# A two-stage kernel (a gated recurrence, then a multiplicative feed-forward): state tiles without zero halves, the diagonal term on TensorE, transposes by DMA, another planner table

## The chip, the cores and the metric

The kernel runs on one core of a Trainium2 chip. The time is the device time of one execution in microseconds; the median of three runs of the kernel before is 220.44 us (220.21 to 220.77). Five engines run side by side, each with its own instruction queue in program order: TensorE (PE), VectorE (DVE), ScalarE (ACT), GpSimd (POOL) and SyncE (SP). POOL and SP also issue the DMA transfers: POOL those that convert f32 to bf16 on the way, SP the others.

## The reference

```python
B, H, S, D = (4, 8, 768, 48)
state = zeros((B, H, D, D))
for t in range(S):
    cur = einsum('bhd,bhe->bhde', u[None] * k[t], v[t])
    y[t] = einsum('bhd,bhde->bhe', r[t], state + cur)
    state = w[t][..., None] * state + einsum('bhd,bhe->bhde', k[t], v[t])
x = y.transpose(0, 2, 1, 3).reshape(B * S, H * D)        # 3072 x 384
out = ((x @ w1) * (x @ w2)) @ w3 @ w_out                 # w1, w2: 384 x 1024, w3: 1024 x 1024, w_out: 1024 x 384
```

## The kernel before

The recurrence is computed in chunks of 128 time steps. Within a chunk the decay is a running sum of logarithms, so that the chunk becomes matrix products: scaled keys times scaled queries (128 x 128 for each batch row and head, strictly causal by a mask), that times v, plus the queries times the state that entered the chunk, plus the diagonal term dv = v * sum(r * u * k).

The work is cut into 12 units (`unit(t)`): 6 chunks of time by 2 pairs of batch rows. A unit holds 2 batch rows x 8 heads x 48 = 768 columns on 128 partitions (time steps). Its steps, by the tile that they write:

- four loads: win (f32, issued by SP), kin, rin and vin (converted to bf16, issued by POOL);
- lw = log w (ACT); cs, the running sum (PE); iw, NEt and Et, three exponentials (ACT); rw, KR's k half and KR's r half, three bf16 products (DVE);
- rk = r*k (DVE, f32), ruk = rk*u (POOL), dg, its sum over 48 (DVE), dv = v*dg (POOL);
- 16 PE transposes of KR into PSUM (L443), one ACT copy of them to KRT (L448);
- per batch row, 8 matmuls of 128 x 128 (L460) and one DVE product with the mask (Mbf, L466); then the matmuls of y (L480 state part, L484 rest), the sum with dv (yb, L491), and PE transposes (L502) and an ACT copy to xT;
- the state: matmuls L519 for two heads at a time, which give a 96 x 96 square of which only the two diagonal 48 x 48 squares are wanted; Tst = that + Sst (DVE, 768 columns); Sbd, the two diagonal squares decayed (POOL, two instructions of 48 partitions); Sst, the whole decayed (POOL, 768 columns).

Two units make a block (`block(n)`, 512 tokens): 8 groups of 3 + 3 matmuls of 512 columns (a, L555, with w1; b, L560, with w2), an ACT copy of a (a_sb, L568), a DVE product (abT, L572); then 4 tiles of 8 matmuls with w34 (L579), an ACT or DVE copy (osb, L586) and a store by SP. The product w34 = w3 @ w_out is made once (`w34_block`): PE transposes of w3 (L354), copies, matmuls with w_out (L366).

Nothing is issued in the order of this text. Each step is declared with an engine, a guessed duration, what it reads and writes, and a priority; `schedule` simulates the engines and always starts the ready step of lowest priority number; the instructions are then issued to the queues in that order. `RANK` shifts the priority of a kind of step, `WEIGHTS_AT` says when each weight is loaded. The planner's numbers set the order alone, never a time on the chip. Between the engines the tile framework puts semaphore waits where data or a buffer needs them. All PSUM is one tile of eight banks (`banks`).

Of the kernel before, what the change touches and what calls it, by code (L numbers as in the profile page):

```python
# [19 lines left out]
    "ne": 35.0, "o": 585.9, "ones": 266.0, "osb": 287.5, "pads": 788.5, "pc": -715.7, "rin": 68.6,  # L20
    "rk": 96.2, "ruk": -33.8, "rw": 700.7, "state": 148.5, "store": -729.5, "table": -999.7, "tr": -53.7,
    "u": 929.4, "vin": 136.2, "w": 156.1, "w3T": 873.0, "win": -499.7, "wm": 844.5, "wt": 733.0, "xT": 70.4,
    "y": 82.9, "yb": -619.8, "yt": -970.4,
}

WEIGHTS_AT = {
    "w1": 9.47, "w2": 28.57, "w3a": 0.47, "w3b": 1.91, "wo": 1.05,
}


class Op:
    __slots__ = ("eng", "dur", "fn", "reads", "writes", "prio", "deps", "tiles", "seq",
                 "start", "end", "lat", "dma", "name", "nleft", "users")

    def __init__(self, eng, dur, fn, reads, writes, prio, lat, dma, name, seq):
        self.eng, self.dur, self.fn = eng, dur, fn
        self.reads, self.writes, self.prio = reads, writes, prio
        self.lat, self.dma, self.name, self.seq = lat, dma, name, seq
        self.deps, self.tiles, self.users = set(), [], []
        self.start = self.end = None  # L40


class Program:
# [39 lines left out]
    def schedule(self, caps):  # L83
# [12 lines left out]
        dma_at = 1500.0  # L96
# [16 lines left out]
        while len(order) < n:  # L113
# [5 lines left out]
            for e, pool in pools.items():  # L119
# [3 lines left out]
                for o in pool:  # L123
                    if ready_at[o] > t or (best is not None and (o.prio, o.seq) >= (best.prio, best.seq)):
                        continue
# [13 lines left out]
                o.start, clock[e] = t, t + o.dur  # L139
                if o.dma:  # L140
                    dma_at = max(dma_at, t + o.dur + 1000.0) + o.dma
                    o.end = dma_at + 1200.0
                else:
                    o.end = t + o.dur
# [6 lines left out]
                for u in o.users:  # L151
                    waiting[u] -= 1
                    lat = 0.0 if (u.eng == e and not o.dma) else o.lat
# [8 lines left out]
            nxt += [f[0] for f in frees if f[0] > t]  # L162
            assert nxt, "the schedule cannot go on"
# [9 lines left out]
def kernel(  # L173
# [27 lines left out]
    NU = NC * NP  # L201
    TB = NP * NB * C
# [18 lines left out]
    KR = many(NS, [C, 2, BH, PAD], BF, "KR")  # L221
    KRT = many(NS, [P, 2, NB, HP, C], BF, "KRT")
    Mbf = many(2 * NS, [C, 2, HP, C], BF, "Mbf")
    rk = many(NS, [C, BH, D], F32, "rk")
    ruk = many(NS, [C, BH, D], F32, "ruk")
    dg = many(NS, [C, BH], F32, "dg")
    dv = many(NS, [C, BH, D], BF, "dv")
    yb = many(2 * NS, [C, DM], BF, "yb")
    pc = many(2 * NP, [P, NB, HP], F32, "pc")
    Tst = many(NP, [P, NB, HP, 2 * D], F32, "Tst")  # L230
    Sst = many(NP, [P, NB, HP, 2 * D], F32, "Sst")
    Sbd = many(NP, [P, NB, HP, 2 * D], BF, "Sbd")
# [16 lines left out]
    u_bc = sb.tile([C, H, D], F32, name="u_bc")  # L249
# [5 lines left out]
    def mm(*cols):  # L255
        return sum(max(n / 2.4 + 2.5, 42.0) for n in cols)

    def act(n):
        return 175 + 0.835 * n

    def dve(n, x=1):
        return 90 + 1.05 * n / x

    def pool(n):
        return 200 + 2.1 * n
# [29 lines left out]
    def c_state():  # L295
        for x in Sbd + Sst:
            nc.vector.memset(x, 0.0)
    op("DVE", 400, c_ones, w=["ones", "LT", "I128"], prio=-10, name="ones")
    op("POOL", 300, c_lt, w=["LT"], prio=-42, name="LT")
    op("POOL", 300, c_id, w=["I128"], prio=-41, name="I128")  # L300
# [3 lines left out]
    op("DVE", 2500, c_state, w=[f"S{i}" for i in range(NP)] + [f"Sbd{i}" for i in range(NP)], prio=-7, name="state0")  # L304
    op("POOL", 1100, c_mask, w=["mask"], prio=-40, name="mask")
    op("SP", 60, lambda: nc.sync.dma_start(u_bc, u.partition_broadcast(C)), w=["u"], prio=-5.0, dma=600.0, name="u")
# [4 lines left out]
    def load(eng, dst, key, src, t, prio, dur):  # L311
        c, p = divmod(t, NP)
        ap = ROW[src][p * NB:(p + 1) * NB, :, c * C:(c + 1) * C, :].rearrange("b h t d -> t (b h) d")
        e = nc.gpsimd if eng == "POOL" else nc.sync
        op(eng, dur, lambda: e.dma_start(dst, ap), w=[key], prio=prio, dma=BH * C * (0.8 if eng == "POOL" else 0.85))  # L315

    def wload(dst, src, key, prio, nbytes):
        op("POOL", 950, lambda: nc.gpsimd.dma_start(dst, src), w=[key], prio=prio, dma=nbytes / 381.0)
# [4 lines left out]
    wor = moe_w_out.rearrange("(gi gp) o -> gp gi o", gp=P)  # L323

# [311 lines left out]
```

## Time and profile before

| | |
|---|---|
| median of the runs | 220.44 us |
| the profiled execution | 221.23 us, of which 219.5 us are the span from first to last instruction |
| PE busy | 165.2 us, 1536 matmuls |
| DVE busy | 147.6 us, 198 instructions |
| POOL busy | 118.5 us, 100 instructions (its DMA issues counted) |
| ACT busy | 108.5 us, 151 instructions |
| DMA | 21.41 MB moved, 27.98 MB read from HBM |

The busy times overlap. An engine's share is a mean over stages: the stretch until the first matmul of a block, and what comes after, have different limits, so the profile is best read stretch by stretch. A POOL row with DMA_DIRECT2D is the time that POOL takes to issue a transfer, not the transfer. The pace of PE is best read from the chain of work, where "x3" rows give three matmuls back to back; the duration of a single matmul includes its latency, of which the next one hides most.

### The profile page before, as it was taken

What the parts mean: (1) busy time and instruction counts of PE and PEld (TensorE: products, weight loads), DVE (VectorE), ACT (ScalarE), POOL (GpSimd) and SP (SyncE); (2) the same over time, 40 slices, a digit from 0 to 9 for tenths busy, and PEclk for the clock granted to TensorE, in tenths of its full rate; (3) what the DMA queues carried; (4) which work ended last, traced back from release to release, by engine and by line L of the source; (5) the groups of instructions that cost most, each with busy time, mean ns of one, the idle gap of its engine ahead of it and who ended that gap; (6) DMA issues with size and microseconds to landing.
All of it is one profiled execution on the core that took longest, in us unless ns stands there. A gap on an engine that the chain in (4) does not pass through costs nothing.

```text
span 219.5 us, 3845 instructions
## 1 busy us (share of the span) xinstructions
PE 165.2 (75%) x1536; PEld 99.9 (46%) x1536; DVE 147.6 (67%) x198; ACT 108.5 (49%) x151; POOL 118.5 (54%) x100
## 2 busy tenths in 40 slices
PE   0060092999457998948899579988879999999993
PEld 0060042676244345535347444476434865464451
DVE  7021014689378299999999999689985698543521
ACT  2061083648570646877458515496534745435410
POOL 7933226189999176976869859766920531000000
PEclk9996557699975599999999999999999999999999
DMA  7999999999999909294669274996280021001033
GB/s 113 181 135 186 153 140 202 138 163 194 160 135 144 139 6 140 75 175 115 36 36 110 73 71 54 105 60 96 21 101 3 0 75 37 3 36 72 0 109 109
DMA packets 105585, 21.41 MB, mean 98 GB/s; under 512 B 99552, under 2 KB 103776, under 8 KB 105568
## 3 DMA queue, kind: packets, MB, share of 16 engines
q0 software_dynamic: 77200, 11.54, 72.7%
q1 hardware_dynamic: 28368, 9.64, 22.1%
q8 instruction: 12, 0.20, 0.4%
q14 instruction: 5, 0.04, 0.1%
HBM read 27.98 MB, written 4.72 MB: 149 GB/s over the span
## 4 chain that ended last, share of the span: by engine, by line
PE 38%; DVE 33%; DMA 10%; issue 9%; POOL 6%; ACT 2%; DVEq 0%; POOLq 0%; ACTq 0%
PE banks L560 11%; DMA vin<-in_v_dram 10%; PE banks L555 10%; DVE Mbf L466 7%; PE banks L579 7%; DVE KR L419 5%; PE banks L443 4%; DVE abT L572 3%; DVE yb L491 3%; DVE rk L425 3%; DVE dg L432 3%; DVE rw L400 3%; PE banks L366 2%; DVE Tst L527 2%; DVE osb L586 1%
## 5 line engine op out<-in xcount | busy, mean ns | idle before, releaser
L572 DVE TENSOR_TENSOR abT<-a_sb,banks 128x512 bf16<-128x512 f32 x48 | 32.5, 682 | 20.1 <-PE banks L560 12.4
L568 ACT COPY a_sb<-banks 128x512 f32<-128x512 f32 x48 | 28.1, 586 | 32.3 <-PE banks L555 32.1
L560 PE MATMUL banks<-xT,w_bf 128*128 128x512 bf16 x144 | 40.3, 389 | 2.2 <-DVE abT L572 2.2
L555 PE MATMUL banks<-xT,w_bf 128*128 128x512 bf16 x144 | 40.4, 390 | 1.0 <-DVE abT L572 0.9
L579 PE MATMUL banks<-w,abT 128*128 128x384 bf16 x192 | 34.0, 326 | 2.2 <-DVE osb L586 2.1
L466 DVE TENSOR_TENSOR Mbf<-banks,mask 128x1024 bf16<-128x1024 f32 x24 | 28.5, 1214 | 4.8 <-PE banks L460 4.8
L428 POOL TENSOR_TENSOR ruk<-rk,u_bc 128x768 f32<-128x768 f32 x12 | 22.5, 1872 | 15.7 <-DVE rk L425 15.6
L534 POOL TENSOR_TENSOR Sbd<-Tst,pc 48x384 bf16<-48x384 f32 x20 | 18.1, 906 | 18.5 <-PE banks L480 17.7
L448 ACT COPY KRT<-banks 128x2048 bf16<-128x2048 bf16 x12 | 22.3, 1867 | 8.9 <-PE banks L443 8.1
L579 PEld LDWEIGHTS <-abT 128*128 128x128 bf16 x192 | 17.9, 98 | 13.3 <-issue 2.3
L560 PEld LDWEIGHTS <-w_bf 128*128 128x128 bf16 x144 | 14.3, 100 | 20.9 <-issue 5.5
L555 PEld LDWEIGHTS <-w_bf 128*128 128x128 bf16 x144 | 14.4, 101 | 18.4 <-issue 3.3
L433 POOL TENSOR_TENSOR dv<-vin,dg 128x768 bf16<-128x768 bf16 x12 | 19.1, 1590 | 4.9 <-issue 2.1
L315 POOL DMA_DIRECT2D vin<-in_v_dram x12 | 14.2, 1185 | 7.6 <-DMA wo_bf<-in_moe_w_out_dram 4.3
L315 POOL DMA_DIRECT2D kin<-in_k_dram x12 | 14.0, 1168 | 7.9 <-DMA vin<-in_v_dram 4.6
L390 PE MATMUL banks<-lw,LT 128*128 128x384 bf16 x24 | 6.5, 356 | 14.0 <-POOL LT L273 12.6
L409 ACT ACTIVATE Et<-banks 128x768 bf16<-128x768 f32 x12 | 9.7, 812 | 14.6 <-PE banks L393 14.6
L508 ACT COPY xT<-banks 128x768 bf16<-128x768 bf16 x12 | 9.6, 802 | 14.0 <-PE banks L502 14.0
L315 POOL DMA_DIRECT2D rin<-in_r_dram x12 | 14.2, 1185 | 3.3 <-DMA rin<-in_r_dram 3.3
L425 DVE TENSOR_TENSOR rk<-rin,kin 128x768 f32<-128x768 bf16 x12 | 13.2, 1102 | 3.7 <-DMA kin<-in_k_dram 3.7
L586 ACT COPY osb<-banks 128x384 f32<-128x384 f32 x12 | 5.8, 481 | 19.4 <-PE banks L579 19.4
L491 DVE TENSOR_TENSOR yb<-banks,dv 128x384 bf16<-128x384 f32 x24 | 12.6, 548 | 4.1 <-POOL dv L433 3.8
(52 smaller groups left out, 260.0 us busy)
## 6 DMA issues: line engine op xcount, KB each, us to landing
win<-in_w_dram SPq DMA_DIRECT2D x12, 384.0 KB, 10.4
out_dram<-osb SPq DMA_DIRECT2D x24, 192.0 KB, 1.9
rin<-in_r_dram POOLq DMA_DIRECT2D x12, 192.0 KB, 7.6
kin<-in_k_dram POOLq DMA_DIRECT2D x12, 192.0 KB, 6.6
vin<-in_v_dram POOLq DMA_DIRECT2D x12, 192.0 KB, 7.8
w_bf<-in_moe_w_dram POOLq DMA_DIRECT2D x2, 1024.0 KB, 19.3
w_bf<-in_moe_w_dram POOLq DMA_DIRECT2D x2, 768.0 KB, 19.4
wo_bf<-in_moe_w_out_dram POOLq DMA_DIRECT2D x1, 768.0 KB, 19.4
```

What stands on the lines that cost most here:

```text
L315: op(eng, dur, lambda: e.dma_start(dst, ap), w=[key], prio=prio, dma=BH * C * (0.8 if eng == "POOL" else 0.85))
L425: op("DVE", dve(BH * D, 2), lambda: nc.vector.tensor_mul(rk[s], rr, kk), r=[kr, kk_], w=[f"rk{s}"], prio=pr + 8)
L428: nc.gpsimd.tensor_mul(ruk[s].rearrange("t (b h) d -> t b h d", b=NB), rk[s].rearrange("t (b h) d -> t b h d", b=NB), u_bc[:, None, :, :]. ...
L433: op("POOL", pool(BH * D), lambda: nc.gpsimd.tensor_mul(dv[s], vv, dg[s][:, :, None].to_broadcast([C, BH, D])), r=[f"dg{s}", kv], w=[f"dv{ ...
L448: nc.scalar.copy(KRTs.rearrange("p x b q t -> p (x b q t)"), o)
L466: nc.vector.tensor_mul(Mbf[m].rearrange("s j q t -> s (j q t)"), o.rearrange("s j f -> s (j f)"), mask.rearrange("s q t -> s (q t)"))
L491: nc.vector.tensor_add(yb[n], banks[:, g.at(Y), :][:, :DM], dv[s][:, b * H:(b + 1) * H, :].rearrange("t h d -> t (h d)"))
L555: nc.tensor.matmul(banks[:, g.at(A), :], lhsT=wt[:, di, fi * P:(fi + 1) * P], rhs=xT[x][:, di, :], start=(di == 0), stop=(di == DI - 1))
L560: nc.tensor.matmul(banks[:, g.at(Bk), :], lhsT=wt[:, di, fi * P:(fi + 1) * P], rhs=xT[x][:, di, :], start=(di == 0), stop=(di == DI - 1))
L568: nc.scalar.copy(a_sb[sa], banks[:, g.at(A), :])
L572: nc.vector.tensor_mul(abT[x][:, fi, :], a_sb[sa], banks[:, g.at(Bk), :])
L579: nc.tensor.matmul(banks[:, g.at(O), :][:, :DM], lhsT=abT[x][:, fi, tt * P:(tt + 1) * P], rhs=w34[:, fi, :], start=(fi == 0), stop=(fi == ...
```

## The change

- **State.** The state keeps two heads one above the other (partitions 0 to 63 and 64 to 127) with 48 columns each, instead of a 96 x 96 square: Tst, Sst and Sbf (formerly Sbd) have 384 columns for a full unit instead of 768. The state matmuls (L758) and the state part of y (L716) are one per head, on halves of the array, 48 columns each: 160 and 160 where there were 80 and 80.
- **Diagonal term.** rk becomes bf16. In units 3 to 12 a DMA transpose issued by SP (L626) turns rk into rkT, six small matmuls with u in block form (u_blk, L633, 8 columns each) give the sums, and a copy of 16 columns (L638) brings them to dg. In units 0 to 2 ruk = rk*u is on DVE in bf16 and the sum stays on DVE. u itself comes through POOL in bf16.
- **Transposes of KR.** In units 6 to 12 two DMA transposes issued by SP (L653) write KRT; the PE transposes and the ACT copy go. Units 0 to 5 keep them.
- **Masks.** For the second batch row of units 5 to 12 ACT copies the product to Mbf (L692) and POOL zeroes it where the mask is zero (affine_select, L695); the other 16 keep the DVE product.
- **Loads.** All loads but the first win go through POOL, in an order that `LOADS` and `STEP` give; w1, w2 are loaded in two halves each, w3 in four quarters.
- **Units and blocks.** The first pair of rows at the first chunk becomes two units of one row (384 columns): 13 units, 8 blocks of 128, 128, 256 and five times 512 tokens. yb, y and its sum are one instruction for both rows. osb copies can go to either engine by a table (`ENGINE`): DVE 5, ACT 19, where there were 12 and 12.
- **Planner.** Other guessed durations, a number for every single step (`STEP`), a model of the port that DVE and POOL share, and two DMA queues in it.

```diff
+STEP = {
+    "table": 6260, "ones": -2200, "LT": -1.5, "pads": -1144, "mask1": 677, "state0": 1306, "mask": 7.5, "u": -10,
...
+LOADS = """win_0 kin_0 rin_0 vin_0 w1_0 w2_0 win_1 kin_1 rin_1 vin_1 u w1_1 w2_1 win_2 kin_2 rin_2 vin_2 wo w3_0 w3_1
+win_3 kin_3 rin_3 vin_3 w3_2 w3_3""".split()
+UNITS = [(0, 0, 1), (0, 1, 1), (0, 2, 2)] + [(c, b, 2) for c in range(1, 6) for b in (0, 2)]
+DMA_KR = set(range(6, 13))
+PE_DIAG = set(range(3, 13))
+POOL_MASK = {(t, 1) for t in range(5, 13)}
+BLOCKS = [[0], [1], [2], [3, 4], [5, 6], [7, 8], [9, 10], [11, 12]]
+SP_LOADS = {("w", 0)}
...
-    rk = many(NS, [C, BH, D], F32, "rk")
+    rk = many(NS, [C, BH, D], BF, "rk")
-    Tst = many(NP, [P, NB, HP, 2 * D], F32, "Tst")
+    Tst = many(NP, [P, NB * HP, D], F32, "Tst")
...
-        op("POOL", pool(BH * D), ruk_, r=[f"rk{s}", "u"], w=[f"ruk{s}"], prio=pr + 8)
+        if t in PE_DIAG:
+            op("SP", 400, lambda: nc.sync.dma_start_transpose(rkTs, rks.rearrange("t h d -> t (h d)")),
...
+                        nc.tensor.matmul(banks[:, g.at(DG), b * H:(b + 1) * H], lhsT=rkTs[:, b * DI + di, :],
+                                         rhs=u_blk[:, di, :], start=(di == 0), stop=(di == DI - 1))
...
+                (nc.scalar.copy if eng == "ACT" else nc.vector.tensor_copy)(dgs, banks[:, g.at(DG), :bh])
...
+        if t in DMA_KR:
+            for x in range(2):
+                def trd(x=x):
+                    nc.sync.dma_start_transpose(KRTs[:, x].rearrange("p b q t -> p (b q) t"),
+                                                KRs[:, x].rearrange("t h d -> t (h d)"))
...
+            if (t, b) in POOL_MASK:
+                op("ACT", act(1024), mcp, r=[MM], w=[f"M{m}"], prio=pr + 7 + b, name=f"mcp_{t}_{b}")
+                op("POOL", 1110, maff, r=[f"M{m}"], w=[f"M{m}"], prio=pr + 7 + b, name=f"maff_{t}_{b}", port=True)
+            else:
+                op("DVE", dve(1024), msk, r=[MM, "mask"], w=[f"M{m}"], prio=pr + 7 + b, name=f"msk_{t}_{b}")
...
-                        nc.tensor.matmul(o[:, b, q * 2 * D:(q + 1) * 2 * D],
-                                         lhsT=KRs[:, 0, h:h + 2, :].rearrange("t h d -> t (h d)"),
-                                         rhs=vv[:, h:h + 2, :].rearrange("t h d -> t (h d)"), start=True, stop=True)
+                        nc.tensor.matmul(o[a:a + PAD, b, h // 2, :], lhsT=KRs[:, 0, b * H + h, :],
+                                         rhs=vv[:, b * H + h, :], start=True, stop=True)
...
-                for e in range(2):
-                    a = e * PAD
-                    nc.gpsimd.tensor_mul(Sbd[p][a:a + D, :, :, e * D:(e + 1) * D].rearrange("p b q e -> p (b q) e"),
+            op("POOL", pool(N // 2), lambda: nc.gpsimd.tensor_mul(Bp, Tp, PCb),
```

How the order moved, at three places. First POOL's queue near the start of the program, from the load of w_out on (w1_bf, w2_bf, w3_bf and wo_bf are the weights; the digit in rin_1 is the buffer). Before:

```order
L318 DMA wo_bf_129<-in_moe_w_out_dram 128x8x384
L315 DMA vin_0_68<-in_v_dram 128x16x48
L315 DMA rin_1_63<-in_r_dram 128x16x48
L315 DMA kin_1_66<-in_k_dram 128x16x48
L318 DMA w3_bf_128<-in_moe_w3_dram 128x4x1024
L315 DMA vin_1_69<-in_v_dram 128x16x48
L315 DMA rin_2_64<-in_r_dram 128x16x48
L315 DMA kin_2_67<-in_k_dram 128x16x48
L315 DMA vin_2_70<-in_v_dram 128x16x48
L273 AFFINE_SELECT LT_133<-LT_133 128x128
L315 DMA vin_3_71<-in_v_dram 128x16x48
L318 DMA w1_bf_126<-in_moe_w1_dram 128x3x1024
```

The same queue from the same load on, now:

```order
L506 DMA wo_bf_129<-in_moe_w_out_dram 128x8x384
L506 DMA w1_bf_126<-in_moe_w1_dram 128x3x512
L450 AFFINE_SELECT mask_134<-mask_134 128x1024
L506 DMA w2_bf_127<-in_moe_w2_dram 128x3x512
L647 TENSOR_TENSOR dv_0_101<-vin_0_68,dg_0_99 128x384
L488 AFFINE_SELECT u_blk_138<-u_blk_138 128x24
L490 AFFINE_SELECT u_blk_138<-u_blk_138 128x24
L502 DMA vin_1_69<-in_v_dram 128x8x48
L506 DMA w1_bf_126<-in_moe_w1_dram 128x3x512
L769 TENSOR_TENSOR Sbf_0_113<-Tst_0_109,pc_0_105 128x192
L506 DMA w2_bf_127<-in_moe_w2_dram 128x3x512
```

The first half of w1 and of w2 now follows w_out directly and stands ahead of three quarters of w3 and of every load of units 3 and later, while POOL's own products (dv, Sbf) of the first units stand between the loads.

Second, SP's queue in the middle of the program. Before (loads of w and stores):

```order
L591 DMA out_0_dram<-osb_1_123 128x384
L315 DMA win_1_73<-in_w_dram 128x16x48
L591 DMA out_0_dram<-osb_2_124 128x384
L315 DMA win_2_74<-in_w_dram 128x16x48
L591 DMA out_0_dram<-osb_3_125 128x384
```

SP's queue now, around units 7 and 8:

```order
L653 DMA_TRANSPOSE KRT_1_90<-KR_1_86 128x8x128 x2
L827 DMA out_0_dram<-osb_3_125 128x384
L626 DMA_TRANSPOSE rkT_0_87<-rk_0_95 128x6x128
L653 DMA_TRANSPOSE KRT_0_89<-KR_0_85 128x8x128
L827 DMA out_0_dram<-osb_0_122 128x384
L827 DMA out_0_dram<-osb_1_123 128x384
L827 DMA out_0_dram<-osb_2_124 128x384
L653 DMA_TRANSPOSE KRT_0_89<-KR_0_85 128x8x128
```

The loads of w have left SP; three transposes of a unit stand in its queue among the stores, and the second transpose of unit 8 stands behind three stores, each of which waits for a finished output tile.

Third, DVE in the second half of the program. Before:

```order
L421 TENSOR_TENSOR KR_1_86<-rw_1_80,Et_1_82 128x16x48
L491 TENSOR_TENSOR yb_0_101<-banks_61,dv_0_99 128x384
L491 TENSOR_TENSOR yb_1_102<-banks_61,dv_0_99 128x384
L400 TENSOR_TENSOR rw_0_79<-rin_1_63,iw_0_77 128x768
L425 TENSOR_TENSOR rk_0_93<-rin_1_63,kin_1_66 128x768
L586 COPY osb_0_122<-banks_61 128x384
L419 TENSOR_TENSOR KR_1_86<-kin_0_65,NEt_1_84 128x16x48
L466 TENSOR_TENSOR Mbf_2_91<-banks_61,mask_134 128x1024
L466 TENSOR_TENSOR Mbf_3_92<-banks_61,mask_134 128x1024
L527 TENSOR_TENSOR Tst_0_109<-banks_61,Sst_0_111 128x768
```

And now:

```order
L638 COPY dg_0_99<-banks_61 128x16
L689 TENSOR_TENSOR Mbf_2_93<-banks_61,mask_134 128x1024
L766 TENSOR_TENSOR Tst_0_109<-banks_61,Sst_0_111 128x384
L807 TENSOR_TENSOR abT_0_120<-a_sb_2_119,banks_61 128x512
L731 TENSOR_TENSOR yb_0_103<-banks_61,dv_0_101 128x2x8x48
L617 TENSOR_TENSOR KR_0_85<-kin_1_66,NEt_0_83 128x16x48
L619 TENSOR_TENSOR KR_0_85<-rw_0_79,Et_0_81 128x16x48
L623 TENSOR_TENSOR rk_1_96<-rin_2_64,kin_2_67 128x768
L689 TENSOR_TENSOR Mbf_0_91<-banks_61,mask_134 128x1024
L597 TENSOR_TENSOR rw_1_80<-rin_2_64,iw_1_78 128x768
```

One mask product a unit instead of two, a copy of 16 columns instead of the sum over 768, half the columns in Tst, and one yb.

459 lines of the change are left out of this document (272 added, 187 removed), and 128 rows, old and new, of tables (ENGINE, RANK, STEP).

## The prediction

> **What bounds the kernel now.** I read the page first, then the busy times by stretch, cut at the first matmul of a block (71 us) and at 160 us, then the chain of waits, then the groups of instructions.
>
> ```profile
> span 219.5 us, 3845 instructions
> PE 165.2 (75%) x1536; PEld 99.9 (46%) x1536; DVE 147.6 (67%) x198; ACT 108.5 (49%) x151; POOL 118.5 (54%) x100
> 0.00:71.00 71.00, 35.00 (x373) 25.14 (x374) 32.84 (x52) 29.67 (x39) 46.08 (x46) 0.80 1.63 157
> 71.00:160.00 89.00, 75.60 (x719) 43.86 (x718) 81.47 (x99) 54.07 (x76) 65.68 (x49) 0.97 0.93 85
> 160.00:219.50 59.50, 54.59 (x449) 30.89 (x447) 33.28 (x49) 24.76 (x36) 6.70 (x7) 1.00 0.18 45
> ```
>
> The last three rows give start and end, length, busy time of PE, weight loads, DVE, ACT and POOL, then PE's clock, the DMA share and GB/s. There are three kernels in one. Up to 71 us no compute engine is full, but the DMA share is 1.63 (two queues at once) at 157 GB/s: transfers bound it. From 71 to 160 us DVE is busy 81.5 of 89 us: DVE bounds it, and PE stands for 13.4 us. After 160 us POOL is nearly done, DVE has slack, and PE is busy 54.6 of 59.5 us: PE bounds it.
>
> What PE has to do is read from the chain, where matmuls stand back to back (start, length, what):
>
> ```profile
> 71.18 1.28 PE banks L555 x3
> 142.22 0.33 PE banks L390 x2
> 142.54 0.18 PE banks L393 x8
> 142.72 0.93 PE banks L443 x16
> 168.15 0.65 PE banks L560 x3
> 171.15 0.20 PE banks L484 x8
> 171.35 0.17 PE banks L480 x4
> 173.07 0.34 PE banks L502 x6
> 173.41 0.33 PE banks L460 x8
> 193.53 1.30 PE banks L579 x8
> 216.01 0.48 ACT osb L586
> ```
>
> A block is sixteen groups of three at 0.65 and four tiles at 1.30: 15.6 us. A unit is 0.51 (running sum) + 0.93 (transposes of KR) + 0.66 (L460) + 0.74 (y) + 0.34 (L502) + 8 state matmuls at L480's 0.17/4 (0.34) = 3.5 us. The first block starts at 71 us (its first three take 1.28 us, half clock), with three units done; six blocks and nine units follow, 93.6 + 31.5 = 125 us, in 148.5 us. The end after PE's last matmul is 3.5 us. So 20 us, 16% of the work, are waits of PE, nearly all before 160 us.
>
> **The change part by part.** The groups (line, engine, shapes, count; busy us, mean ns; idle before) that carry the prices:
>
> ```profile
> L572 DVE TENSOR_TENSOR abT<-a_sb,banks 128x512 bf16<-128x512 f32 x48 | 32.5, 682 | 20.1 <-PE banks L560 12.4 <-ACT a_sb L568 3.3 <-ACT lw L383 2.6
> L466 DVE TENSOR_TENSOR Mbf<-banks,mask 128x1024 bf16<-128x1024 f32 x24 | 28.5, 1214 | 4.8 <-PE banks L460 4.8
> L428 POOL TENSOR_TENSOR ruk<-rk,u_bc 128x768 f32<-128x768 f32 x12 | 22.5, 1872 | 15.7 <-DVE rk L425 15.6
> L448 ACT COPY KRT<-banks 128x2048 bf16<-128x2048 bf16 x12 | 22.3, 1867 | 8.9 <-PE banks L443 8.1 <-DVE Mbf L466 0.6 <-PE banks L480 0.2
> L534 POOL TENSOR_TENSOR Sbd<-Tst,pc 48x384 bf16<-48x384 f32 x20 | 18.1, 906 | 18.5 <-PE banks L480 17.7
> L425 DVE TENSOR_TENSOR rk<-rin,kin 128x768 f32<-128x768 bf16 x12 | 13.2, 1102 | 3.7 <-DMA kin<-in_k_dram 3.7
> L433 POOL TENSOR_TENSOR dv<-vin,dg 128x768 bf16<-128x768 bf16 x12 | 19.1, 1590 | 4.9 <-issue 2.1 <-DVE dg L432 1.4 <-POOL Sbd L534 0.8
> L540 POOL TENSOR_TENSOR Sst<-Tst,pc 128x768 f32<-128x768 f32 x8 | 12.0, 1496 | 0.2
> L432 DVE TENSOR_REDUCE dg<-ruk 128x16 f32<-128x768 f32 x12 | 11.3, 944 | 5.8 <-POOL ruk L428 5.7
> L527 DVE TENSOR_TENSOR Tst<-banks,Sst 128x768 f32<-128x768 f32 x10 | 9.5, 948 | 0.7 <-PE banks L519 0.6
> L586 DVE COPY osb<-banks 128x384 f32<-128x384 f32 x12 | 6.6, 550 | 7.2 <-PE banks L579 7.2
> L359 ACT COPY w3T<-banks 128x1024 bf16<-128x1024 bf16 x4 | 4.1, 1013 | 12.2 <-PE banks L354 11.0 <-PE banks L366 1.2
> L281 POOL TENSOR_SCALAR_AFFINE_SELECT mask<-mask 128x1024 bf16<-128x1024 bf16 x1 | 1.1, 1107 | 0.1
> ```
>
> DVE: eight masks go (8 x 1.21 = -9.7); nine to ten of the sums L432 go (-9.3); Tst halves (948 to the 550 of a 384-column read of PSUM: -3.9); seven osb copies go to ACT (-3.9); rk in bf16 costs 0.55 instead of 1.10 (row below; -6, or 0 if it waits for POOL); ruk of three units comes (+1.2); abT in small blocks pays its fixed part oftener: 550 at 384 and 682 at 512 columns give 0.28 at 128, so 16 x 0.28 + 8 x 0.41 for 8 x 0.68, +2.3. Sum -29 (bound -23): 147.6 becomes about 118.
>
> There is a second gain. DVE products of two bf16 tiles in SBUF wait for a POOL product in progress, but not for POOL issuing a DMA:
>
> ```profile
> 108.86 1.20 POOL L315 DMA_DIRECT2D rin<-in_r_dram  x1
> 109.86 0.55 DVE L400 TENSOR_TENSOR rw<-rin,iw 128x768 bf16<-128x768 bf16 x1
> 117.61 1.72 POOL L433 TENSOR_TENSOR dv<-vin,dg 128x768 bf16<-128x768 bf16 x1 [0.39 <-DVE yb L491]
> 117.90 1.84 DVE L400 TENSOR_TENSOR rw<-rin,iw 128x768 bf16<-128x768 bf16 x1
> ```
>
> The same product takes 0.55 us in one place and 1.84 in the other, where it ends as POOL's dv ends. POOL's products fall from 72 us (ruk 22.5, Sbd 18.1, Sst 12.0, dv 19.1) to some 44: ruk gone, Sbd and Sst half, and eight masks (8 x 1.11) come. Whether a mask on POOL holds DVE up no row shows: at worst each costs one product 1.1 us (+8.9 on DVE), at best nothing; I take half, within the waits below.
>
> POOL: -22.5 (ruk) - 9 (Sbd) - 6 (Sst) + 8.9 (masks) + 12 x 1.20 (issuing win) + about 4 (weights in more pieces, small units) = -10. ACT: 7 copies to KRT go (-13.1), 8 mask copies of 1024 columns come (at L359's 1.01: +8.1), 7 osb (+3.4), small blocks (+2.6): +1. Neither is the bound: 108 and 110 of some 187 us.
>
> PE: seven units' transposes go (-6.5); 60 tiny matmuls come (at L393's 0.18/8: +1.4); 48-column matmuls by pairs in y and state at L484's 0.025 (160 of them for 80 at 0.043 in each: +1.2 together); small blocks at the 0.058 of a 128-column transpose for 0.054: +0.4. Sum -3.5: PE's work hardly changes. So the gain must come from an earlier start and from fewer waits.
>
> The start. Sizes of transfers (KB each, median us to landing):
>
> ```profile
> win<-in_w_dram SPq DMA_DIRECT2D x12, 384.0 KB, 10.4
> out_dram<-osb SPq DMA_DIRECT2D x24, 192.0 KB, 1.9
> vin<-in_v_dram POOLq DMA_DIRECT2D x12, 192.0 KB, 7.8
> w_bf<-in_moe_w_dram POOLq DMA_DIRECT2D x2, 1024.0 KB, 19.3
> w_bf<-in_moe_w_dram POOLq DMA_DIRECT2D x2, 768.0 KB, 19.4
> ```
>
> Before, w1 and w2 (768 KB each) are issued after w3 and four units' tiles. Now the first halves follow u, a quarter of w3, loads of units 0 to 2 without vin of 1 and 2, and w_out: 3776 KB, 24.6 us at the measured 157 GB/s, so the first block can start near 27 us. PE's queue then holds both 128-token blocks and the rest of the w3 work; it can reach the first output tile only when the last quarter of w3 has landed: 7328 KB, 48 us at 157 GB/s, 50 us on the clock. Behind that stand 8 us of PE work ahead of the first output tile (two w3 transposes of 8, three products of 1.30 with w_out, y and steps of units 3 to 5). First output tile: 58 us. If one queue moves the bytes faster it is 53, if POOL holds loads back it is later (second rival).
>
> From there PE has left: 22/24 of all a and b (264 x 0.217 = 57.2), 24 output tiles (31.2), 8.6 units x 3.5 less the seven transposes plus the additions (26): 114. Waits: in the stretch where DVE had slack PE lost 1.4 of 56 us (4.9 idle less the 3.5 at the end), 2.5%; in all after 71 us 16%. DVE will be loaded to some 67% (118 less the 33 before, of 126 us), but queues in order on SP and POOL now carry transposes and masks that PE waits for. I take 10%, 11.4 us; the ends give 3 and 19.
>
> The moved transposes: KRT took 0.93 of PE + 1.87 of ACT; now two transfers of 256 KB and one of 192 KB a unit, queued on SP behind stores that wait for output tiles, and the L460 matmuls, then every PE step behind them, wait. No row shows a DMA transpose. Bounds for the 704 KB: at 157 GB/s 4.6 us, at a store's pace (192 KB in 1.9) 7 us, at a vin's (192 KB in 7.8 from issue to landing, one after another) 29 us. I take 5 to 7, since a store moves without conversion too; that hides behind the 14.6 us that a unit then has.
>
> Sum: 58 + 114.3 + 11.4 + 3.5 = 187.2 us of span. The profiled execution had 219.5 of span in 221.23 us, the median of the runs is 220.44, so 0.9 over the span: **188 us**.
>
> **Rivals.**
> - The late DMA bound. After 50 us remain 9 x 960 KB of loads, 24 x 192 of stores, 5504 of transposes: 19.2 MB, 122 us at 157 GB/s, ending at 172: hidden. If a transpose moves at half that pace, 36 us more: 208 + 1. For it: the share is already 1.63 in the start. Against: the second stretch needs only 85 GB/s.
> - The start is not shortened: POOL now issues all loads and its products wait in the same queue; if blocks go on steadily only at 71 us as before, 13 us more: 201.
> - Slower than before: the transposes go one 128 x 128 piece after another. Up to the old end there are 219.5 - 3.5 - 58 = 158 us for 8.6 units, 19.3 for each of the last seven; loads and stores take 8.8 of that, so it decides at 10.5 us of transposes a unit. At vin's 29 us it would be 58 + 23 + 7 x 29 = 284 us and more. For it: 22 pieces a unit, each of small rows. Against: a load with rows as small runs at 157 GB/s when several are in flight.
>
> The Trainium skill speaks to both sides of this: "VectorE: DVE Perf Modes", section "The three transpose paths", gives 1309 ns for a 128 x 128 transpose by DMA against 390 ns on TensorE, which taken 22 times in a row is an estimated 29 us a unit, the slow rival. "Advanced Engine Details and Errata", section "X-Bar Transpose (TRN2)", says that such transfers are as fast as regular ones, which is the forecast. No run here shows either.
>
> **Chances.** Forecast 0.70 (own range 178 to 197: waits at 3 and 19 us), late start 0.12 (201), late DMA 0.12 (up to 209), slow transposes 0.06 (over 220). The range for 8 in 10 is 176 to 206. About 0.3% (0.7 us) is what can be told from no change: faster 0.93, same 0.01, slower 0.06.
>
> **What would show it.** Right: the first 128-column block matmuls near 27 us, the first output tile at 53 to 60 us, DVE near 118 us with its two-tile products mostly at 0.55, PE over 85% busy from then on. Wrong: L460's successor waiting for DMA KRT in units 6 to 12, SP transposes that land 10 us after issue, a DMA share over 0.9 after 60 us, or PE idle for POOL's dv or Mbf.

## The result and the profile after

The changed kernel takes 198.4 us (median of 195.9, 198.2, 198.5 and 198.6), the kernel before on the same chip 220.6: a ratio of 0.896, interval 0.889 to 0.904. The profiled execution took 198.6 us with a span of 196.9. A median here and below is of all four executions of a kernel, while a ratio counts only those within 1.5% of its fastest, which leaves out the profiled executions of thin_transposes (185.4 us) and of state_products_doubled (197.5 us). The forecast was 188: the direction is right and the time lies in the range, but a third of the 32 us did not come.

From the page of the kernel after (busy times, the DMA share in 40 slices, the two data queues, the chain by line):

```profile
span 196.9 us, 4315 instructions
PE 161.3 (82%) x1740; PEld 97.9 (50%) x1740; DVE 117.8 (60%) x191; ACT 108.4 (55%) x187; POOL 110.3 (56%) x111
DMA  5999999999999999999999999999981570140033
q0 software_dynamic: 79520, 16.16, 101.3%
q1 hardware_dynamic: 27680, 10.56, 34.5%
PE 53%; DMA 28%; POOL 6%; DVE 5%; ACT 4%; issue 2%; SPq 0%; POOLq 0%; DVEq 0%; ACTq 0%
```

The busy times are those of the forecast (118, 110, 108 for DVE, ACT and POOL; PE 161.7). What is new is the third line: the transfers are busy without a gap through slice 29, some 143 us, and 28% of the chain is DMA. Of the two data queues q0 holds what POOL issues (loads) and q1 what SP issues (transposes, stores); the profile gives both as a share of the same 16 DMA engines. "The queue of transfers" below means what stands in both. The same stretch of 50 us before and after (start and end, length, PE, weight loads, DVE, ACT, POOL, PE's clock, DMA share, GB/s):

```profile
100.00:150.00 50.00, 42.18 (x398) 24.43 (x393) 47.15 (x58) 28.98 (x43) 38.30 (x30) 1.00 0.91 72
100.00:150.00 50.00, 42.08 (x448) 22.29 (x447) 31.36 (x42) 25.24 (x44) 27.52 (x25) 0.97 1.57 142
```

In the first row, of before, DVE is full (47.2 of 50) and the transfers have room (72 GB/s). In the second DVE stands for 19 us, the transfers carry twice as much, and PE is no busier than before. The bound has moved from DVE to the queue of transfers.

Where PE and the chain stand for it (chain: start, length, what; then PE's timeline: one product with w_out at full pace, three waits, the first two with the row behind them, and POOL's wait; then two stretches of one microsecond, columns as above):

```profile
44.32 9.52 DMA rkT<-rk
64.88 6.67 DMA rkT<-rk
112.98 15.55 DMA rin<-in_r_dram
131.64 14.19 DMA KRT<-KR
```

```profile
45.12 1.46 PE L556 MATMUL banks<-wo_bf,w3T 128*128 128x384 bf16 x8
53.88 0.32 PE L633 MATMUL banks<-u_blk,rkT 128*128 128x8 bf16 x6 [4.64 <-DMA rkT<-rk]
54.06 2.72 PE L556 MATMUL banks<-wo_bf,w3T 128*128 128x384 bf16 x8
137.97 0.31 PE L633 MATMUL banks<-u_blk,rkT 128*128 128x8 bf16 x6 [3.64 <-DMA rkT<-rk]
138.13 2.60 PE L796 MATMUL banks<-xT,w_bf 128*128 128x512 bf16 x6
145.87 0.40 PE L683 MATMUL banks<-KRT 64*128 64x128 bf16 x8 [2.19 <-DMA KRT<-KR]
54.56 1.47 POOL L647 TENSOR_TENSOR dv<-vin,dg 128x768 bf16<-128x768 bf16 x1 [6.60 <-DVE dg L638]
```

```profile
52.00:53.00 1.00, 0.00 (x0) 0.00 (x0) 0.00 (x0) 0.00 (x0) 0.00 (x0) 0.97 0.81 40
55.00:56.00 1.00, 1.00 (x5) 0.49 (x4) 1.00 (x2) 0.00 (x0) 1.00 (x2) 0.50 4.05 146
```

A transpose that is issued at 44.32 us has landed at 53.84. PE waits 4.64 us for it, and the eight matmuls with w_out behind it then take 2.72 us where others take 1.46: after the wait PE's clock is down to 0.50. POOL's dv of that unit waits 6.60 us for the sum, and with it the loads that stand behind it in POOL's queue, so that between 50 and 53 us the transfers themselves fall to some 60 GB/s. The same wait comes again at 138 us.

### The profile page after: what moved, and what is told of

Read it like the earlier page. It is cut to its first block, busy times and chain, and to the rows that moved or that the text cites. A ratio compares the mean times of both kernels' runs of the same rounds, so it can differ in the third digit from the quotient of the medians.

```text
span 196.9 us, 4315 instructions
## 1 busy us (share of the span) xinstructions
PE 161.3 (82%) x1740; PEld 97.9 (50%) x1740; DVE 117.8 (60%) x191; ACT 108.4 (55%) x187; POOL 110.3 (56%) x111
## 4 chain that ended last, share of the span: by engine, by line
PE 53%; DMA 28%; POOL 6%; DVE 5%; ACT 4%; issue 2%; SPq 0%; POOLq 0%; DVEq 0%; ACTq 0%
PE banks L814 13%; PE banks L796 11%; PE banks L791 10%; DMA rkT<-rk 8%; DMA rin<-in_r_dram 8%; DMA KRT<-KR 7%; PE banks L556 5%; DMA vin<-in_v_dram 5%; PE banks L683 3%; PE banks L722 3%; PE banks L665 2%; PE banks L716 2%; PE banks L544 1%; POOL vin L502 1%; PE banks L758 1%
## 5 line engine op out<-in xcount | busy, mean ns | idle before, releaser
L803 ACT COPY a_sb<-banks 128x512 f32<-128x512 f32 (+2 forms) x64 | 30.0, 482 | 33.8 <-PE banks L791 24.6
L807 DVE TENSOR_TENSOR abT<-a_sb,banks 128x512 bf16<-128x512 f32 (+2 forms) x64 | 33.9, 549 | 19.7 <-PE banks L796 13.4
L796 PE MATMUL banks<-xT,w_bf 128*128 128x512 bf16 (+2 forms) x192 | 40.1, 333 | 0.3 <-ACT a_sb L803 0.2
L791 PE MATMUL banks<-xT,w_bf 128*128 128x512 bf16 (+2 forms) x192 | 38.0, 329 | 0.7 <-DVE abT L807 0.6
L647 POOL TENSOR_TENSOR dv<-vin,dg 128x768 bf16<-128x768 bf16 (+1 forms) x13 | 18.3, 1410 | 20.6 <-DVE dg L638 8.4
L796 PEld LDWEIGHTS <-w_bf 128*128 128x128 bf16 x192 | 16.3, 98 | 13.8 <-issue 1.5
L695 POOL TENSOR_SCALAR_AFFINE_SELECT Mbf<-Mbf 128x1024 bf16<-128x1024 bf16 x8 | 9.0, 1121 | 23.0 <-ACT Mbf L692 23.0
L731 DVE TENSOR_TENSOR yb<-banks,dv 128x768 bf16<-128x768 f32 (+1 forms) x13 | 11.5, 894 | 8.5 <-PE banks L722 7.2
L556 PE MATMUL banks<-wo_bf,w3T 128*128 128x384 bf16 x64 | 14.6, 384 | 0.2 <-DVE w3T L549 0.2
L502 POOL DMA_DIRECT2D win<-in_w_dram x12 | 14.0, 1170 | 0.0
L747 ACT COPY xT<-banks 128x768 bf16<-128x768 bf16 (+1 forms) x13 | 9.8, 753 | 6.3 <-PE banks L742 6.3
L580 ACT ACTIVATE lw<-win 128x768 bf16<-128x768 f32 (+1 forms) x13 | 10.3, 803 | 5.0 <-DMA win<-in_w_dram 4.9
L683 PE MATMUL banks<-KRT 64*128 64x128 bf16 x192 | 9.5, 232 | 4.1 <-DMA KRT<-KR 2.2
## 6 DMA issues: line engine op xcount, KB each, us to landing
out_dram<-osb SPq DMA_DIRECT2D x24, 192.0 KB, 1.9
rin<-in_r_dram POOLq DMA_DIRECT2D x11, 192.0 KB, 8.2
kin<-in_k_dram POOLq DMA_DIRECT2D x11, 192.0 KB, 7.0
vin<-in_v_dram POOLq DMA_DIRECT2D x11, 192.0 KB, 8.7
```

The source lines that it names most:

```text
L502: op(eng, 60 if eng == "SP" else 700 + 250 * nb, lambda: e.dma_start(dst[:, :nb * H], ap), w=[key], prio=turn_of(f"{src}in_{t}"), dma=nb * ...
L556: nc.tensor.matmul(o[:, :DM], lhsT=w3T[fi % 2][:, gi, :], rhs=wo_bf[:, gi, :], start=(gi == 0), stop=(gi == FI - 1))
L580: op("ACT", act(N), lambda: nc.scalar.activation(LW[:, :, :D], ww, Act.Ln), r=[kw, "table"], w=[f"lw{s}"], prio=pr, name=f"ln_{t}")
L647: op("POOL", pool(N), lambda: nc.gpsimd.tensor_mul(dvs, vv, dgs[:, :, None].to_broadcast([C, bh, D])), r=[f"dg{s}", kv], w=[f"dv{s}"], pri ...
L683: nc.tensor.matmul(o[:, e, q, :], lhsT=KRTs[a:a + PAD, 0, b, q, :], rhs=KRTs[a:a + PAD, 1, b, q, :], start=True, stop=True)
L731: nc.vector.tensor_add(ybs.rearrange("t b (q e d) -> t e (b q) d", e=2, d=D), o, dvs.rearrange("t (b q e) d -> t e (b q) d", b=nb, e=2))
```

## Experiments

In all of them the priority of a step is its place in a list of names, so that the order can be held or changed at will:

```diff
-        o = Op(eng, dur, fn, tuple(r), tuple(w), prio + RANK.get(kind, 0.0) + STEP.get(name, 0.0), dma, name, kind,
+        o = Op(eng, dur, fn, tuple(r), tuple(w), NEW.get(name, AT.get(name, 0.0)), dma, name, kind,
```

With the changed kernel's own list (AT) its order comes back step for step; a step that comes anew (NEW) stands where the one that it replaces stood. Theories at the outset: A, transposes that wait in a full queue make PE wait; B, the bytes in the queue set the pace, whosesoever they are; C, a transpose has a fixed price of 7 us.

| run | median us | ratio to before, interval |
|---|---|---|
| changed kernel | 198.4 | 0.896 (0.889 to 0.904) |
| thin_transposes | 184.2 | 0.825 (0.820 to 0.830) |
| thin_loads | 184.6 | 0.835 (0.828 to 0.842) |
| sum_on_dve_to_unit4 | 198.5 | 0.897 (0.891 to 0.902) |
| no_dma_transposes | 194.1 | 0.874 (0.869 to 0.880) |
| no_transposes_replanned | 192.5 | 0.872 (0.868 to 0.876) |
| last_three_units_by_dma | 193.7 | 0.878 (0.875 to 0.882) |
| two_chunk_units_throughout | 189.1 | 0.857 (0.854 to 0.859) |
| all_masks_on_dve | 189.4 | 0.857 (0.853 to 0.861) |
| three_parts_undone | 183.2 | 0.829 (0.826 to 0.832) |
| three_parts_undone_other_order | 186.9 | 0.841 (0.835 to 0.847) |
| state_products_doubled | 196.0 | 0.873 (0.866 to 0.881) |
| weights_late | 180.5 | 0.817 (0.814 to 0.819) |

### Less in the queue, same order

**thin_transposes** (the first two lines fill rkT once, at the start).

```diff
-        for x in Sst:
+        for x in Sst + rkT:
...
-            op("SP", 400, lambda: nc.sync.dma_start_transpose(rkTs, rks.rearrange("t h d -> t (h d)")),
+            op("SP", 400, lambda: nc.sync.dma_start_transpose(rkTs[:, :1], rks.rearrange("t h d -> t (h d)")[:, :P]),
...
-                    nc.sync.dma_start_transpose(KRTs[:, x].rearrange("p b q t -> p (b q) t"),
-                                                KRs[:, x].rearrange("t h d -> t (h d)"))
+                    nc.sync.dma_start_transpose(KRTs[:, x].rearrange("p b q t -> p (b q) t")[:, :1],
+                                                KRs[:, x].rearrange("t h d -> t (h d)")[:, :P])
```

> The order of every engine is that of the changed kernel (198.4 us); each DMA transpose carries only its first 128x128 block (1 of 6 of rk, 1 of 8 of each half of KR), the rest of rkT and KRT is stale, so r.(u k) and the products with KR are not the reference's. Theory A, transposes that wait in a full DMA queue cost the missing 10 us: PE's waits for rkT at 53.9 (4.64 us) and 138 us (3.64) and for KRT at 145.9 (2.19) go, and with them the half clock behind each (some 1.3 + 0.6 us at 54, 1.1 + 0.4 at 138): the first output tile at 58 to 60 instead of 66.4 us, 184 to 190 us in all. Theory B, the queue is full of loads, whose bytes set the end: the transposes land 2 us sooner at most, 194 to 198. Theory C, a transpose has a fixed price of about 7 us whatever it carries: it lands after 7 us as before, 196 to 199.

**thin_loads.**

```diff
-        e = nc.sync if eng == "SP" else nc.gpsimd
+        e, n = nc.sync if eng == "SP" else nc.gpsimd, 8 if t >= 6 else C
...
-        op(... lambda: e.dma_start(dst[:, :nb * H], ap), ...
+        op(... lambda: e.dma_start(dst[:n, :nb * H], ap[:n]), ...
```

> Same order again; from unit 6 on each load of w, k, r and v carries 8 of its 128 partitions, so the later units compute on old rows (not the reference's result). Full transposes. Theory A: the queue is free after some 75 us, transposes from then on land in 2 to 3 us instead of 7, the waits at 138 and 146 us and rin's 15.5 us go, the wait at 54 us stays: 189 to 193. Theory B (bytes of loads set the late stage): below 187. Theory C (fixed price of a transpose): they still land after 7 us, 196 to 199.

Both give back 14 us: 184.2 and 184.6. That is A's size for the one and B's for the other, so the two theories are one: loads and transposes share the 16 engines, and taking bytes out on either side is enough. The stretch from 100 to 150 us, first with thin transposes, then with thin loads:

```profile
100.00:150.00 50.00, 49.55 (x505) 26.18 (x501) 36.35 (x51) 31.97 (x55) 27.23 (x24) 1.00 0.97 94
100.00:150.00 50.00, 50.00 (x507) 26.33 (x507) 35.70 (x52) 32.23 (x55) 21.41 (x24) 1.00 0.58 106
```

PE is busy 49.6 and 50.0 us where it was 42.1. How long a transpose takes is the queue's doing as well: the median from issue to landing of KRT and rkT in the changed kernel, then with thin loads, where they carry as much as before:

```profile
KRT<-KR SPq DMA_TRANSPOSE x14, 7.3
rkT<-rk SPq DMA_TRANSPOSE x10, 7.2
KRT<-KR SPq DMA_TRANSPOSE x14, 3.8
rkT<-rk SPq DMA_TRANSPOSE x10, 3.1
```

So C falls in this form. But with thin transposes a block of 128 x 128 alone, an eighth or a sixth of the bytes, still needed 4.2 us (KRT) and 4.4 us (rkT) in the median, more than a whole one beside thin loads. The first of them, issued at 43.5 us, landed after 7.9 us where the whole one had taken 9.5, and PE's wait for it was 3.06 us at 51.5: a small transpose waits for the other transfers under way too.

### Parts of the transposes undone, same order

**sum_on_dve_to_unit4.**

```diff
-PE_DIAG = set(range(3, 13))
+PE_DIAG = set(range(5, 13))
```

> r.(u k) of units 3 and 4 goes back to DVE (a product of 0.55 and a sum of 0.94 us each, as units 0 to 2 have it); the other units keep their transposes and the steps their order. Theory A: PE has no wait of 4.64 us at 49 us, POOL's dv 3 and the loads behind it go 5 us sooner, the first output tile at 58 to 61 us; 190 to 194 in all. Rival: PE and POOL wait there for the last quarter of w3 and for loads anyway, and DVE's 3 us more delay KR: first output tile at 65 us or later, 197 to 201.

Half of A came true: the first output tile stands at 59.7 us instead of 66.4. The total is the rival's, 198.5. They are given back at one place (chain, then DVE's and PE's timeline of this run):

```profile
106.93 16.50 DMA rin<-in_r_dram
123.62 0.56 DVE L623 TENSOR_TENSOR rk<-rin,kin 128x768 bf16<-128x768 bf16 x1 [7.78 <-DMA rin<-in_r_dram]
125.77 2.72 PE L814 MATMUL banks<-w,abT 128*128 128x384 bf16 x8 [7.19 <-DVE abT L807]
```

A tile of r, issued at 106.9, lands at 123.4. DVE's rk waits 7.78 us for it, the last abT of a block stands behind rk in DVE's queue, and PE waits 7.19 us for abT, again with half the clock behind it (eight matmuls in 2.72 us). An earlier start doesn't help here: the loads of the late units come no sooner than the bytes ahead of them.

**no_dma_transposes.**

```diff
-DMA_KR = set(range(6, 13))
-PE_DIAG = set(range(3, 13))
+DMA_KR = set()
+PE_DIAG = set()
```

> All transposes by DMA are undone: KR of units 6 to 12 by PE and an ACT copy (PE +6.5, ACT +13 us), r.(u k) of units 3 to 12 by DVE (+14 us); the steps keep their order otherwise. Theory A: no wait for DMA is left, but PE, ACT and DVE get their work back: DVE 131, ACT 121, PE 164 us busy. If the transposes cost about what they save, 196 to 201. If what they save on DVE and ACT is worth more than their waits (rival): 203 to 212. If they cost more than they save: 190 to 195.

194.1, 4 us faster than the changed kernel, in an order that was made for the other work: in this kernel the transposes cost more than they save. PE, ACT and DVE have their work back (DMA share by slices, busy times, and the stretch from 100 to 150 us):

```profile
PE 164.3 (85%) x1792; PEld 103.4 (54%) x1792; DVE 131.5 (68%) x205; ACT 120.1 (62%) x189; POOL 109.5 (57%) x109
DMA  4999999999999999999999990190002100230033
100.00:150.00 50.00, 48.91 (x540) 28.47 (x538) 38.59 (x54) 36.18 (x56) 24.53 (x21) 1.00 0.64 65
```

Busy in all is 13.7 us more on DVE and 11.7 more on ACT, and the kernel is faster: the queue is through at about 115 us instead of 143, and PE is busy 48.9 of the 50 us.

### Other parts of the change, without DMA transposes

From here the order, and which of DVE and ACT copies w3T, w34, osb, were planned anew for each kernel by the kernel's own planner, which goes by its guessed durations.

**no_transposes_replanned** (the same edit, a new order).

> The kernel without DMA transposes (194.1 us) with its order of steps, and the engines of w3T, w34 and osb copies, planned anew for that work by the kernel's own planner. What it computes is the reference's. In 194.1 PE lost 5.8 us between 60 and 100 us to steps that stood in the wrong order (DVE's Mbf and KR, ACT's KRT and a_sb). Theory A (what is left there is order): 186 to 191. Rival: DVE, busy 36.6 of 40 us there, is the bound, which no order changes: 193 to 196.

192.5, between the two: inconclusive. Between 60 and 100 us PE is still busy only 34.0 of 40 us.

**last_three_units_by_dma.**

```diff
-DMA_KR = set(range(6, 13))
-PE_DIAG = set(range(3, 13))
+DMA_KR = set(range(10, 13))
+PE_DIAG = set(range(10, 13))
```

> As the re-planned one, but the transposes of KR and rk of units 10 to 12 by DMA: the queue has nothing to do by then (share 0.13 to 0.55 after 115 us in the kernel without transposes). PE -2.8, ACT -5.6, DVE -4.5 us. Theory A (a transpose costs only where the queue is full): they land in 2 to 4 us, no PE wait for KRT or rkT over 1 us, 1 to 4 us under the re-planned kernel: 184 to 190. Theory C (a price of 7 us each wherever they stand): as slow as the re-planned kernel or slower by up to 3 us.

193.7: not faster than without. The transposes land in 4.0 (KRT) and 4.3 us (rkT, medians), and no wait of PE for them shows, yet PE is busy only 45.8 us between 100 and 150, where the re-planned kernel has 49.3; its longest waits are now at osb (2.15) and xT (1.42). Whether these are the transposes' doing or the order's this run doesn't tell.

**two_chunk_units_throughout.**

```diff
-UNITS = [(0, 0, 1), (0, 1, 1), (0, 2, 2)] + [(c, b, 2) for c in range(1, 6) for b in (0, 2)]
+UNITS = [(c, b, 2) for c in range(6) for b in (0, 2)]
-POOL_MASK = {(t, 1) for t in range(5, 13)}
+POOL_MASK = {(t, 1) for t in range(4, 12)}
-BLOCKS = [[0], [1], [2], [3, 4], [5, 6], [7, 8], [9, 10], [11, 12]]
+BLOCKS = [[2 * n, 2 * n + 1] for n in range(6)]
```

> No DMA transposes, units of two batches throughout and six blocks of 512 tokens, as before the change, planned anew; the rest of the change stays. Theory: the blocks of 128 tokens fill PE while transfers bound the start: without them the first a/b matmul comes at 42 to 48 us instead of 30, and two 24ths of a, b and o (some 7.9 us of PE) move behind 60 us: 4 to 8 us slower than the re-planned kernel. Rival: PE had that room before 60 us anyway, or later waits take the gain back: within 2 us of it.

189.1: 3.4 us faster, where 4 to 8 us slower were expected. (The eight masks on POOL stay, with the units' new numbers.) The a/b matmuls start at 41.8 us (L796) instead of 25.0 and the first output tile stands at 65.9 instead of 55.1, as expected; the end comes sooner all the same.

**all_masks_on_dve.**

```diff
-POOL_MASK = {(t, 1) for t in range(5, 13)}
+POOL_MASK = set()
```

> No DMA transposes, all masks as products on DVE, as before the change, planned anew. DVE +9.7 (some 141 us busy), ACT -8.1, POOL -9.0. Theory, DVE is near its limit between 60 and 130 us: 4 to 8 us slower than the re-planned kernel. Rival, masks on POOL hold up DVE's two-tile products by as much as they take off it: within 2 us of it, with fewer of those products stretched beyond 0.55 us.

189.4: 3.1 us faster, where slower was expected. Busy times, first with half of the masks on POOL (the re-planned kernel), then with all on DVE:

```profile
PE 162.2 (85%) x1778; PEld 101.6 (53%) x1792; DVE 131.8 (69%) x208; ACT 116.7 (61%) x186; POOL 109.4 (57%) x109
PE 161.0 (86%) x1777; PEld 101.7 (54%) x1792; DVE 135.3 (72%) x212; ACT 113.2 (60%) x182; POOL 100.6 (54%) x101
```

Eight masks of 1.22 us came back to DVE, but its busy time rose by 3.5 us, not 9.7. DVE's products of two bf16 tiles took 3.7 us less in sum, while 8.8 us went from POOL; the other 2.5 us are four copies that the new plan gives to ACT.

**three_parts_undone** and **three_parts_undone_other_order** (the last two edits and no_dma_transposes together, in two orders).

> No DMA transposes, all masks on DVE and units of two batches throughout, planned anew; of the change remain the state without empty halves, rk in bf16 with the products on DVE, the loads on one queue with weights in pieces, and w3's and the output's copies shared by ACT. If the two gains seen against the re-planned kernel (192.5) are of the parts (3.4 by units, 3.1 by masks) they add up: 184 to 187. If they were luck of the order (rival), it comes out anywhere between 187 and 193.

> The same work in another order, which the planner holds for as good (0.6 us longer by its own account). It measures what an order is worth that differs by chance. Theory, order is a detail: within 1 us of the other. Rival: 2 to 4 us apart, and then differences of 3 us between re-planned kernels prove nothing of a part.

183.2 and 186.9: the two gains add up, and another order that the planner holds for as good is 3.7 us away. So a difference of 3 us between two re-planned kernels shows nothing of a part: that small units or masks on POOL each cost 3 us is not shown. That both together don't pay is, as far as two orders on each side can show it: with them the same work took 194.1 and 192.5 us, without them 186.9 and 183.2.

**state_products_doubled** (on three_parts_undone; the diff shows the products alone, Tst and Sst likewise; the matmuls and DVE's sum keep their width).

```diff
-    Sbf = many(NP, [P, NB * HP, D], BF, "Sbf")
+    Sbf = many(NP, [P, NB * HP, 2 * D], BF, "Sbf")
...
-            PCb = PC[:, :, None].to_broadcast([P, nb * HP, D])
+            PCb = PC[:, :, None].to_broadcast([P, nb * HP, 2 * D])
```

> As three_parts_undone, but GpSimd's products for the state run over tiles of twice the width, as before the change (Sbf and Sst 128x768 instead of 128x384; the sum on DVE stays at 384), planned anew. POOL +15 us (101 to 116 busy, 62% of the span). Theory, POOL has room and only its share of stretched DVE products grows: 0.5 to 3 us slower. Rival, POOL issues all loads, its products hold them back: 4 us slower or more.

The ratio is 0.873 for 0.829, 10 us of 221, and 7 us above the slowest of the three other kernels with this work (0.841). Its page, then that of three_parts_undone:

```profile
PE 166.8 (85%) x1696; PEld 98.3 (50%) x1696; DVE 146.1 (75%) x192; ACT 110.5 (56%) x157; POOL 109.8 (56%) x94
PE 156.9 (86%) x1696; PEld 93.9 (52%) x1696; DVE 131.1 (72%) x189; ACT 110.1 (61%) x158; POOL 97.2 (54%) x94
```

POOL is busy 12.6 us more, and so is DVE, by 15.0, though its work hardly changed (the memsets of the wider tiles). In sum its five products of two tiles took 51.3 us here against 38.9; in the two other orders with POOL at 97.2 us it was 43.9 and 43.1, so 7 to 12 us go with the doubled products. Between 60 and 100 us three things come together (PE's and POOL's timeline, then two stretches of this run, columns as above):

```profile
63.97 1.04 PE L665 MATMUL banks<-I,KR 128*128 128x128 bf16 x8 [3.62 <-DVE KR L619]
64.65 1.16 POOL L502 DMA_DIRECT2D win<-in_w_dram  x1
72.93 1.47 POOL L769 TENSOR_TENSOR Sbf<-Tst,pc 128x768 bf16<-128x768 f32 x1 [7.12 <-PE banks L716]
74.35 1.19 POOL L502 DMA_DIRECT2D kin<-in_k_dram  x1
64.00:68.00 4.00, 3.38 (x21) 1.64 (x22) 3.97 (x7) 2.45 (x2) 1.81 (x2) 0.50 1.60 138
68.00:73.00 5.00, 5.00 (x62) 2.58 (x61) 3.24 (x6) 3.38 (x6) 0.07 (x1) 0.50 0.10 26
```

PE had waited 3.62 us for DVE's KR and runs at a clock of 0.50; POOL's next Sbf waits for PE; the loads behind it wait too, and the queue of transfers, which is the bound in this stretch, carries 26 GB/s. These rows are of an execution of 197.5 us. The two that the ratio counts took 192.0 and 194.5, and how much of these waits they have too is open.

**weights_late** (on three_parts_undone; the diff shows the new condition alone, and the calls stand behind the first units' loads in the program).

```diff
-        op("POOL", 950, lambda: nc.gpsimd.dma_start(dst, src), w=[key], prio=turn_of(key), dma=nbytes / 381.0, name=key)
+        op("POOL", 950, lambda: nc.gpsimd.dma_start(dst, src), r=["vin3", "w3_3"] if key[:2] in ("w1", "w2") else [], w=[key], prio=turn_of(key), dma=nbytes / 381.0, name=key)
```

> As three_parts_undone, but w1 and w2 are loaded after all of w3 and the tiles of units 0 to 3, about as before the change, planned anew: first a/b matmul at 53 to 60 us. By the prediction's reasoning (what starts later ends later): 8 to 14 us slower than three_parts_undone. Rival: before 60 us PE is given the units' and w3's work instead, and its sum of work after that hardly grows: within 2 us.

180.5, the fastest of all, where 8 to 14 us slower were expected. Of this run the first and last start of the a/b and output matmuls and the first 60 us; then the same three rows of three_parts_undone:

```profile
L791 PE MATMUL banks<-xT,w_bf x144: 376/379/390, 50.9 to 167.6; 128*128 128x512 bf16 x144
L814 PE MATMUL banks<-w,abT x192: 322/326/337, 69.7 to 174.8; 128*128 128x384 bf16 x192
0.00:60.00 60.00, 42.45 (x555) 29.65 (x556) 47.01 (x67) 40.20 (x52) 52.15 (x55) 1.00 1.69 172
L791 PE MATMUL banks<-xT,w_bf x144: 376/379/390, 36.7 to 167.5; 128*128 128x512 bf16 x144
L814 PE MATMUL banks<-w,abT x192: 322/326/337, 65.9 to 177.3; 128*128 128x384 bf16 x192
0.00:60.00 60.00, 40.40 (x489) 27.32 (x490) 42.01 (x64) 37.25 (x50) 50.66 (x54) 0.97 1.69 177
```

The a/b matmuls start 14 us later, the first output tile 4 us later, and the end is 2.5 us sooner: before 60 us PE does as much (42.5 against 40.4 us), only other work, that of the units. The delay is smaller than it looks: in three_parts_undone only 12 matmuls of a (2.9 us) ran before 50.9 us, and the first b matmul (L796) starts at 52.1 us there and at 52.8 here. How much of the 2.7 us is the weights and not the order stays open; that a kernel can start its a/b matmuls at 50.9 us and be no slower is shown.

## Why the prediction was right or wrong

**The start: right in its first number, wrong in its second.** The first block began at 30.0 us (27 forecast). The first output tile stood at 66.4, not 58. The bytes of w3 were not late; the transpose of rk of unit 3 was, with half the clock behind it. With one block in each transpose it is 63.1 us, without that transpose 59.7, without any 58.6. The rival of the late start (201) comes nearest in number, but sum_on_dve_to_unit4 speaks against it: with the start repaired the time stays at 198.5.

**The transposes, "hidden behind the 14.6 us that a unit then has": the step that failed.** It set the end of all transfers (172 us) against the end of the kernel. But a load or a transpose is due when the instruction that needs it stands at the head of its engine's queue, and while the transfers are busy without a gap, up to 143 us, each one lands late: 7.2 us after issue for a transpose, up to 16 for a tile of r. thin_transposes puts the price of their bytes at 14 us in the same order of steps, and thin_loads gives back as much. With it taken off, the changed kernel would take 184, so the rest of the sum was, if anything, 4 us too long. Nearest to this is the rival of the late DMA bound, to which I gave 0.12: transfers did bind, but by when each one lands, not by their end, which came at 143 us and not at 172, and its time (209, by a transpose at half the pace) did not come. Of the signs set down as wrong, three showed: a DMA share of 1.82 from 60 to 143 us, transposes that landed up to 14.2 us after issue, and PE's waits for them.

**The engines' work: right.** DVE, ACT, POOL and PE are within 3 us of the forecast. From the first output tile to PE's end it took 126.9 us for the forecast 125.7, of which PE was busy 117.7. That the two agree is luck. The same stretch of the changed kernel, then of thin_transposes:

```profile
66.36:193.25 126.89, 117.68 (x1208) 65.75 (x1204) 80.94 (x114) 74.04 (x126) 60.41 (x54) 0.99 1.21 128
63.06:179.99 116.93, 115.12 (x1209) 65.38 (x1205) 81.34 (x114) 74.12 (x126) 60.78 (x54) 1.00 1.01 99
```

With the transposes' bytes gone PE stands for 1.8 us in it, with them for 9.2. The forecast's 11.4 us of waits, a tenth of the work, were for queues and masks; they are about the size of the price that the transposes were not given. So in the sum the miss shows elsewhere: of the 9.7 us by which the span is longer than 187.2, 8.4 are the first output tile.

**DVE's products and POOL: right in kind, too good in size.** In the changed kernel rw and rk take 0.62 us, but the two halves of KR 0.96 and 1.03, not "mostly 0.55". Doubling the state products on POOL brought DVE 7 to 12 us in such products and cost the kernel 7 to 10 of the 38 us by which three_parts_undone beats the kernel before. So the halved products are the one part of the change whose worth is measured beyond the 3.7 us of an order, though in a single order of the doubled kernel, and the prediction had them inside the waits only. For the masks I took half (4.5 of 8.9 us); measured were 3.7 of 8.8, which is no more than two orders of the same work differ by. The Trainium skill, "SBUF — State Buffer", section "SBUF: two separate sides", says that VectorE and GpSimd share a pair of ports that one instruction holds for its whole length; these runs agree, with 7 to 12 us more in DVE's two-tile products for 12.6 us more of POOL.

**The slow transposes** (one piece after another, 29 us a unit) didn't come: 256 KB landed in 3.8 us once the loads were thin, and 192 KB in 3.1, against 1.9 for a store of 192 KB. Of the Trainium skill's two statements that the prediction set against each other, the one of "Advanced Engine Details and Errata", section "X-Bar Transpose (TRN2)", came nearer: between 60 and 143 us rkT, 192 KB, took 7.0 us (median), a store of 192 KB through the same SP queue 5.9 and a load of 192 KB of r through POOL's 8.2. The 29 us estimated from "VectorE: DVE Perf Modes", section "The three transpose paths", no run shows.

**The sum itself** was built on the first output tile plus the work that remains, as if what starts later ended later. two_chunk_units_throughout and weights_late contradict that: with output tiles 11 and 4 us later their spans are 3.7 and 2.5 us shorter. That is no more than two orders of the same work differ by, so it shows no gain, but the loss isn't there either. PE has units' work to do in the meantime. It seems better to let the sum go by PE's busy time up to a given time (40 to 42 us of the first 60 in these kernels, 37.3 in the changed one, 28.5 before) than by the first instruction of a kind; no forecast here was made so.

**What stays open:** the shares of bf16 rk, of the single load queue, and of the copies moved to ACT in the gain, none of which was run alone, and the few us that belong to the order. What the table does show is that with the three parts undone the changed kernel is 11 to 15 us faster.

## What to carry to other kernels

Before moving work from an engine to DMA, look at the DMA share of the stretch in which it will run, and add its bytes to those that must land before the last unit starts: a transfer is hidden if it is through when its reader's turn comes, not when the kernel ends. Work taken from GpSimd can also shorten VectorE's two-tile products, here by 7 to 12 us for 12.6 us of GpSimd. And measure two orders of the same work before a difference of 2% is put down to a part of a change.

## What was not expected of the hardware

Beside many loads a transpose of 128 x 1024 took 7.3 us to land (median), and one of a single 128 x 128 block 4.2 to 4.4 with the other transposes thin as well; beside few loads the large one took 3.8. After waits of 3.6 to 7.2 us PE's clock was 0.50 for 4 to 6 us (eight matmuls of 384 columns in 2.72 us for 1.46), so that by these figures such a wait cost 2 to 3 us more than its length; after the wait of 2.19 us at 145.9 it stayed at 1.00.
